# Window attention in front of two gated layers on one Trainium2 core: the first batch's attention, with scores two items ahead, later scaling and an earlier release

## The chip, the cores and the metric

The kernel runs on 1 core of a Trainium2 chip. The metric is the time of one execution on the device, in microseconds; three runs of the kernel before stand in the table below. The engines are called PE (TensorE, matrix products into PSUM banks), PEld (PE's weight loads), DVE (VectorE), ACT (ScalarE), POOL (GpSimd) and SP (SyncE, which issues the transfers).

## The reference

Three stages follow each other; each one's output is the next one's input.

```python
# q, k, v: (4 batches, 8 heads, 576 rows, 64)
rel = pos[:, None] - pos[None, :]
bias = slopes[:, None, None] * (-np.abs(rel).astype(np.float32))[None, :, :]
mask = (rel >= 0) & (rel < window)            # window = 128
scores = np.where(mask, scale * q @ k.T + bias, -1e9)
attn = np.exp(scores - scores.max(-1)); attn = attn / (attn.sum(-1) + 1e-09)
x = (attn @ v)                                # to (2304, 512)
...
g = x @ w_gate                                # 512 -> 1536
silu = g * (1.0 / (1.0 + np.exp(-g)))
x = silu * (x @ w_val) @ w_out
...
h = x @ w_in2                                 # 512 -> 2048
out = (h * np.cos(h)) @ w_out2
```

The weights of the last two stages come in 64 bits and are turned into float32 on the chip; products use a high and a low part of each operand (`wh`, `wl`, `xh`, `xl`), three matmuls for one.

## The kernel before

The instructions of all engines are written out in program order by one Python loop, and each engine works its own queue in that order; waits are set by tile. The loop over `n` runs through 144 *items* of attention: 16 units (4 batches of 4 pairs of heads, `u`), each of 9 items, which are blocks of 128 rows (four for either head, `i` = 0 to 3, and a tail of 64 rows for both heads together). Two neighbouring items form a group, `first` and `final` are its first and last place. For each item these steps stand in the loop at fixed lags:

- `do_s`: scores by PE into a bank of the pool `s` (two banks), in bursts of two groups at places 0 and 4 of a unit and the tail at place 7 (`AHEAD`); each burst needs K and q of its unit, transposed by PE (`prep_t`, lines L401 and L413, into the bank `pq` or `t`) and copied into SBUF by DVE or ACT (`prep_q` L407, `prep_k` L410, `prep_tail` L421 and L423).
- `do_bias` (L471, DVE): adds the slope and forms the row maximum, from PSUM into `e`.
- `do_exp` (L480, ACT): the exponential with its row sum, two items behind the first of the group.
- `do_guard` and `do_recip` (L486 and L491, DVE) on the row sums, and `do_norm` (L503 and L504, POOL): scaling, `NORM` = 2 items behind the group's last.
- `do_t` (L513 and L523, PE): transposes, 5 behind; `do_hi` (L541 and L536, ACT): copies out of PSUM, 6 behind; `do_pv` (L576, and L554 and L556 for the tail, PE): product with v, 8 behind for the blocks, 9 for the tail. Its end writes `xh` (ACT, L581 and L563) and `xl` (DVE, L582 and L565).

When the fourth pair of a batch has its tail's `xl`, `release` frees the batch for the *filler*: matmuls of the gated layer for the first three slices of 128 of its 1536 columns (`a_l1`, `a_l2`, lines L81 to L83 into the pool `pm`, two banks). `run_fill` puts 1.6 steps of three matmuls each into every item. Until the first release there is nothing to fill in. In program order the first release falls at item 45.

The weights of these slices, nine blocks of 512 columns, are converted during the first batch: `convert` loads a block (L92, L97), ACT makes two parts of it (L123, L125), DVE clamps, shifts and joins them (L126, L133, L134), DVE or POOL adds (L138 or L143), ACT or POOL makes the high part `wh` (L165, L170), POOL the low part `wl` (L158).

Behind the attention the rest of the filler, the other slices of the gated layer and the cosine layer follow; their code is not changed.

Of the kernel before, what the change touches and what calls it, by code (L numbers as in the profile page):

```python
# [28 lines left out]
def kernel(  # L29
# [70 lines left out]
    def convert(dst, todo, fast=False, act=False):  # L100
# [9 lines left out]
        added = set()  # L110
        for i, (key, src, f, column, pool) in enumerate(todo):
# [3 lines left out]
            if act and i + 1 < len(todo):  # L115
                stages.append(load_stage(*todo[i + 1][1:4]))
# [3 lines left out]
            if wide:  # L120
                t = conv_p.tile([128, 512], F32, tag="ct", name="ct")
                r = st[:, :, 0]
                nc.scalar.activation(out=t, in_=st[:, :, 1].bitcast(F32), func=AF.Abs, scale=65536.0)  # L123
                yield
                nc.scalar.activation(out=r, in_=r, func=AF.Copy, scale=2.0 ** -29)  # L125
                nc.vector.tensor_scalar(t, t, LEAST_HIGH, GREATEST_HIGH, ALU.max, ALU.min)  # L126
                yield
# [3 lines left out]
            if wide:  # L131
                ti = t.bitcast(U32)
                nc.vector.tensor_scalar(ti, ti, 3, None, ALU.logical_shift_left)  # L133
# [98 lines left out]
    def evac_l1(nm, f, st, ps):  # L232
        if nm == "g":
# [94 lines left out]
    s_p = att.enter_context(tc.tile_pool(name="s", bufs=8))  # L328
# [51 lines left out]
    load_qk(1)  # L380
    load_v(0)
# [3 lines left out]
    for t in qtx:  # L385
        nc.vector.memset(t, 0.0)
    pth = {}
# [21 lines left out]
    def prep_k(u):  # L409
        nc.vector.tensor_copy(out=KT[u][:, :NB * 128], in_=PQ.pop((u, "k")))  # L410
# [5 lines left out]
    def prep_tail(u):  # L416
        ps = PQ.pop((u, "t"))
        KT[u] = qk_p.tile([128, S], F32, tag="kx", name="kx")
# [21 lines left out]
    def do_s(groups):  # L440
# [36 lines left out]
    def do_exp(n):  # L477
        w = width(items[n][2])
        e, (st, m) = E[n], ST[n]
        nc.scalar.activation(out=e[:, :w], in_=e[:, :w], func=AF.Exp, bias=st[:, m:m + 1], scale=-1.0,  # L480
                             accum_out=st[:, 2 + m:3 + m])

    def do_guard(g):
        st = ST[g[0]][0]
        c = len(g)
        nc.vector.tensor_scalar(st[:, 4:4 + c], st[:, 2:2 + c], 1e-9, None, ALU.add)  # L486

    def do_recip(g):
        st = ST[g[0]][0]
        c = len(g)  # L490
        nc.vector.reciprocal(out=st[:, 6:6 + c], in_=st[:, 4:4 + c])  # L491
# [6 lines left out]
    def do_norm(n):  # L498
# [5 lines left out]
        nc.gpsimd.tensor_scalar(e[:, :w], e[:, :w], st[:, 6 + m:7 + m], 1.0, ALU.mult, ALU.mult)  # L504
# [108 lines left out]
    EXP, NORM, TRANS, HIGH, PVS = 2, 2, 5, 6, 8  # L613
    AHEAD = {0: (0, 2), 4: (4, 6), 7: (8,)}
    Q0, K0, TT0 = 2, 5, 4
    due = pdue = 0.0
    for n in range(N + PVS + 2):
# [11 lines left out]
        if ended(HIGH):  # L629
            do_hi(ended(HIGH))  # L630
# [4 lines left out]
        if ended(NORM):  # L635
            do_guard(ended(NORM))
        if ended(TRANS):
            do_t(ended(TRANS))
        if v1 is not None:
            if idx == TT0:  # L640
                g = ended(TRANS)
                prep_tail_t(v1, TT[g[0]] if g else ps_t.tile([128, 512], F32, tag="t", name="t"))
        if ended(NORM):
            do_recip(ended(NORM))
            for m in ended(NORM):
# [5 lines left out]
        for back in (PVS, PVS + 1):  # L651
            for m in (ended(back) or ())[-1:]:
                u_, h_, i_ = items[m]
                if back == PVS and h_ == 1 and i_ == NB - 1 or back == PVS + 1 and i_ == NB:
                    do_pv(m)
        if v1 is not None:
# [10 lines left out]
            if idx == max(TT0, K0) + 1:  # L667
# [555 lines left out]
```

## Time and profile before

| | |
|---|---|
| runs | 993.61 us median of 3 (993.47 to 993.85) |
| the profiled execution | 993.59 us, span 991.6 us |
| PE busy | 968.4 us (98%), 5616 instructions |
| DVE, ACT, POOL busy | 745.7 us (75%), 587.0 us (59%), 477.9 us (48%) |
| mean granted clock of PE | 0.984 |
| chain that ended last | PE 89%, DVE 4%, ACT 2% |

The span runs from the first to the last instruction; the execution's own time is some 2 us longer. An engine's busy share is an average over stages that differ: the profile's slices show PE's clock at 0.7 to 0.8 in the first three of forty and at the full value in those behind. [...]

### The profile page before, as it was taken

To read this page: it belongs to the slowest core of one execution; us is meant where nothing else is said; L and a number is where in the kernel's file an instruction comes from. 1 tells how busy PE (TensorE), PEld (TensorE's weight loads), DVE (VectorE), ACT (ScalarE), POOL (GpSimd) and SP (SyncE) were. 2 spreads that over 40 slices of the span, in tenths; PEclk is the share of its full clock that TensorE was granted. 3 is DMA by queue.
4 is the path that set the end of the run, shared out by engine and by line. 5 is a ranking of instruction groups with operands and counts; after the bars stand their busy time and mean duration, and the time that the engine had idled before them with its cause. 6 is when DMAs were issued, how large, how long until landed. Compare 5 with 4: busy or idle time off the path is not lost.

```text
span 991.6 us, 17044 instructions
## 1 busy us (share of the span) xinstructions
PE 968.4 (98%) x5616; PEld 888.0 (90%) x5616; DVE 745.7 (75%) x1560; ACT 587.0 (59%) x1349; POOL 477.9 (48%) x563
## 2 busy tenths in 40 slices
PE   5889999999999999999999999999999999999998
PEld 3568888889999999999999999888889888898886
DVE  6978877866288988989989755889666796666664
ACT  5876666554244545555555433877677776776663
POOL 4766556642245667669679720344222342223221
PEclk8879999999999999999999999999999999999999
DMA  7533333222373646647557625765767656676552
GB/s 180 139 100 73 97 79 91 72 80 70 106 282 106 202 128 216 209 128 251 172 165 242 203 81 174 285 202 176 249 199 229 200 162 200 184 242 200 164 177 85
DMA packets 145159, 163.65 MB, mean 165 GB/s; under 512 B 64688, under 2 KB 105648, under 8 KB 144816
## 3 DMA queue, kind: packets, MB, share of 16 engines
q1 hardware_dynamic: 143872, 162.27, 52.5%
q8 instruction: 45, 0.74, 0.3%
q10 hardware_dynamic: 1200, 0.30, 0.1%
q14 instruction: 42, 0.34, 0.1%
HBM read 126.88 MB, written 35.65 MB: 164 GB/s over the span
## 4 chain that ended last, share of the span: by engine, by line
PE 89%; DVE 4%; ACT 2%; issue 1%; DMA 1%; POOL 1%; SPq 1%; POOLq 0%; DVEq 0%; ACTq 0%
PE l L81 13%; PE l L83 13%; PE l L82 13%; PE pm L81 8%; PE pm L83 7%; PE pm L82 7%; PE pm L946 6%; PE pm L948 5%; PE pm L947 5%; PE s L463 4%; PE pv L576 3%; PE t L523 1%; PE pq L401 1%; PE t L513 1%; DVE cs L765 1%
## 5 line engine op out<-in xcount | busy, mean ns | idle before, releaser
L1071 POOL TENSOR_TENSOR r<-r,c 128x384 f32<-128x384 f32 x96 | 104.2, 1087 | 261.9 <-ACT r L1069 174.8
L81 PE MATMUL pm<-xh,wh 128*128 128x384 f32 (+1 forms) x452 | 150.9, 334 | 0.0
L83 PE MATMUL pm<-xh,wl 128*128 128x384 f32 (+1 forms) x452 | 144.8, 320 | 0.0
L82 PE MATMUL pm<-xl,wh 128*128 128x384 f32 (+1 forms) x452 | 144.6, 320 | 0.0
L81 PE MATMUL l<-wo,hh 128*128 128x512 f32 x288 | 113.9, 395 | 0.0
L82 PE MATMUL l<-wo,hh 128*128 128x512 f32 x288 | 113.5, 394 | 0.0
L83 PE MATMUL l<-wo,hl 128*128 128x512 f32 x288 | 113.5, 394 | 0.0
L946 PE MATMUL pm<-xh,ws 128*128 128x384 f32 x318 | 107.7, 339 | 0.5 <-ACT q L1097 0.5
L767 POOL TENSOR_TENSOR cs<-cs,st 128x512 uint32<-128x512 uint32 x56 | 79.9, 1427 | 57.6 <-DVE cs L765 48.8
L948 PE MATMUL pm<-xh,ws 128*128 128x384 f32 x318 | 107.6, 338 | 0.0
L947 PE MATMUL pm<-xl,ws 128*128 128x384 f32 x318 | 107.1, 337 | 0.0
L504 POOL TENSOR_SCALAR e<-e,st 128x128 f32<-128x128 f32 (+1 forms) x144 | 60.6, 424 | 63.2 <-DVE st L491 38.9
L81 PEld LDWEIGHTS pm<-xh,wh 128*128 128x128 f32 x452 | 85.1, 188 | 3.2 <-issue 3.2
L82 PEld LDWEIGHTS pm<-xl,wh 128*128 128x128 f32 x452 | 85.3, 189 | 0.0
L83 PEld LDWEIGHTS pm<-xh,wl 128*128 128x128 f32 x452 | 85.0, 188 | 0.0
L1061 ACT ACTIVATE a<-c 128x384 f32<-128x384 f32 x96 | 49.7, 518 | 54.6 <-DVE c L1087 54.6
L1066 DVE SCALAR_TENSOR_TENSOR r<-a,r 128x384 f32<-128x384 f32 x96 | 76.0, 792 | 3.3
L480 ACT ACTIVATE e<-e,st 128x256 f32<-128x256 f32 (+1 forms) x144 | 67.9, 473 | 16.3 <-DVE st L471 12.3
L1068 ACT ACTIVATE r<-r 128x384 f32<-128x384 f32 x96 | 50.3, 524 | 42.7 <-DVE r L1066 42.7
L81 PE MATMUL l<-uh,wh 128*128 128x384 f32 x216 | 72.8, 337 | 0.7 <-DVE acc L892 0.5
L83 PE MATMUL l<-uh,wl 128*128 128x384 f32 x216 | 72.6, 336 | 0.0
L82 PE MATMUL l<-ul,wh 128*128 128x384 f32 x216 | 72.5, 336 | 0.0
(171 smaller groups left out, 2622.6 us busy)
## 6 DMA issues: line engine op xcount, KB each, us to landing
ws<-wid SPq DMA_DIRECT2D x168, 256.0 KB, 2.8
wo<-wod SPq DMA_DIRECT2D x48, 512.0 KB, 5.0
st<-in_moe_w_out_dram SPq DMA_DIRECT2D x28, 512.0 KB, 3.8
st<-in_moe_w_in_dram SPq DMA_DIRECT2D x16, 512.0 KB, 3.7
st<-in_moe_w_gate_dram SPq DMA_DIRECT2D x12, 512.0 KB, 4.1
st<-in_moe_w_val_dram SPq DMA_DIRECT2D x12, 512.0 KB, 4.0
wid<-sh SPq DMA_DIRECT2D x24, 256.0 KB, 4.1
wid<-sl SPq DMA_DIRECT2D x24, 256.0 KB, 3.6
```

The costliest lines, as they stand in the source:

```text
L81: nc.tensor.matmul(out=ps, lhsT=ah, rhs=bh, start=start, stop=False)
L82: nc.tensor.matmul(out=ps, lhsT=ah, rhs=bl, start=False, stop=False)
L83: nc.tensor.matmul(out=ps, lhsT=al, rhs=bh, start=False, stop=stop)
L480: nc.scalar.activation(out=e[:, :w], in_=e[:, :w], func=AF.Exp, bias=st[:, m:m + 1], scale=-1.0, accum_out=st[:, 2 + m:3 + m])
L504: nc.gpsimd.tensor_scalar(e[:, :w], e[:, :w], st[:, 6 + m:7 + m], 1.0, ALU.mult, ALU.mult)
L767: nc.gpsimd.tensor_tensor(out=ti, in0=ti, in1=st[:, :, 0], op=ALU.add)
L946: nc.tensor.matmul(out=o, lhsT=wh, rhs=xh_, start=start and kk == 0, stop=False, skip_group_check=True)
L947: nc.tensor.matmul(out=o, lhsT=wh, rhs=xl_, start=False, stop=False, skip_group_check=True)
L948: nc.tensor.matmul(out=o, lhsT=wl, rhs=xh_, start=False, stop=kk == 1, skip_group_check=True)
L1066: nc.vector.scalar_tensor_tensor(out=r, in0=a, scalar=-C2, in1=r, op0=ALU.mult, op1=ALU.add)
L1068: nc.scalar.activation(out=r, in_=r, func=AF.Abs)
L1071: nc.gpsimd.tensor_tensor(out=r, in0=r, in1=h, op=ALU.mult)
```

## The change

The loop over items stays; what changes is at which item the steps stand, which engine makes one copy, and in which shape some small instructions work.

- Units of the first batch get their scores two items earlier (`bursts`), into four banks: groups take turns between the pool `s` and the pool `pm`, which the filler does not use yet.
- Guard and scaling stand 3 items behind a group's last in place of 2, except for the last pair of the first batch (`staged`), which keeps 2 and has its transposes, copies and products one, one and two items earlier.
- The row statistics lie in ten fixed tiles of 12 columns; sums stand in columns 2 and 4, and the guard and the reciprocal of two items run over three columns, the one between included.
- K is copied by ACT in place of DVE. In the first batch q and K are transposed at places 1 and 3 of a unit in place of 2 and 5, and the next q and k are loaded at place 2 in place of 6.
- The clamp and the shift of a converted block go over even and odd words in turn (`p (c t) -> p t c`); the second block is loaded before the first v.
- Value rows of the filler wait for the silu of their own slice alone.
- In program order the first release falls at item 42.

```diff
@@ convert
         stages = [load_stage(*todo[0][1:4])]
         added = set()
+        if act:
+            yield
+            stages.append(load_stage(*todo[1][1:4]))
...
-                nc.vector.tensor_scalar(t, t, LEAST_HIGH, GREATEST_HIGH, ALU.max, ALU.min)
+                w = t.rearrange("p (c t) -> p t c", t=2) if act else t
+                nc.vector.tensor_scalar(w, w, LEAST_HIGH, GREATEST_HIGH, ALU.max, ALU.min)
...
-                nc.vector.tensor_scalar(ti, ti, 3, None, ALU.logical_shift_left)
+                w = ti.rearrange("p (c t) -> p t c", t=2) if act else ti
+                nc.vector.tensor_scalar(w, w, 3, None, ALU.logical_shift_left)
@@ a_l1, evac_l1
-            while (nm, f) not in g0 or (nm == "v" and "silu" not in st):
+            while (nm, f) not in g0 or (nm == "v" and ("silu", f) not in st):
...
-                if f == F0 - 1:
-                    st["silu"] = True
+                st["silu", f] = True
@@ before the loop
     load_qk(1)
+    next(pieces)
     load_v(0)
...
+    stats = [const.tile([128, 12], F32, name=f"st{j}") for j in range(10)]
+    for t in stats:
+        nc.vector.memset(t, 1.0)
@@ prep_k
-        nc.vector.tensor_copy(out=KT[u][:, :NB * 128], in_=PQ.pop((u, "k")))
+        if u not in KT:
+            KT[u] = qk_p.tile([128, S], F32, tag="kx", name="kx")
+        nc.scalar.copy(out=KT[u][:, :NB * 128], in_=PQ.pop((u, "k")))
@@ do_s
-            ps = ps_s.tile([128, 512], F32, tag="s", name="s")
-            st = s_p.tile([128, 8], F32, tag="st", name="st")
+            if items[g[0]][0] < NP and stat_turn[0] % 2:
+                ps = pm.tile([128, 512], F32, tag="pm", name="pm")
+            else:
+                ps = ps_s.tile([128, 512], F32, tag="s", name="s")
+            st = stats[stat_turn[0] % len(stats)]
+            stat_turn[0] += 1
@@ do_guard, do_recip
-        c = len(g)
-        nc.vector.tensor_scalar(st[:, 4:4 + c], st[:, 2:2 + c], 1e-9, None, ALU.add)
+        c = 2 * len(g) - 1
+        nc.vector.tensor_scalar(st[:, 5:5 + c], st[:, 2:2 + c], 1e-9, None, ALU.add)
...
-        nc.vector.reciprocal(out=st[:, 6:6 + c], in_=st[:, 4:4 + c])
+        nc.vector.reciprocal(out=st[:, 8:8 + c], in_=st[:, 5:5 + c])
@@ the loop over items
-    EXP, NORM, TRANS, HIGH, PVS = 2, 2, 5, 6, 8
-    AHEAD = {0: (0, 2), 4: (4, 6), 7: (8,)}
-    Q0, K0, TT0 = 2, 5, 4
+    EXP, NORM, TRANS, HIGH, PVS = 2, 3, 5, 6, 8
+    bursts = {}
+    for u in range(U):
+        when = (-2, 2, 5) if u < NP else (0, 4, 7)
+        for at, js in zip(when, ((0, 2), (4, 6), (8,))):
+            bursts.setdefault(max(u * NI + at, 0), []).extend(first[u * NI + j] for j in js)
+    TT0 = 4
...
+    def last_pair(n):
+        return 0 <= n < N and items[n][0] == NP - 1
+    def staged(n, late, early):
+        if last_pair(n - early) and n - early in final:
+            return final[n - early]
+        return None if last_pair(n - late) else final.get(n - late)
...
+        Q0, K0 = (1, 3) if u < NP - 1 else (2, 5)
...
+        normal, turned, high = staged(n, NORM, 2), staged(n, TRANS, 4), staged(n, HIGH, 5)
...
-        if u < U and idx in AHEAD:
-            do_s([first[u * NI + j] for j in AHEAD[idx]])
+        if n in bursts:
+            do_s(bursts[n])
...
-        for back in (PVS, PVS + 1):
+        for back in (PVS + 1, PVS, PVS - 2):
...
-                if back == PVS and h_ == 1 and i_ == NB - 1 or back == PVS + 1 and i_ == NB:
+                if (h_ == 1 and i_ == NB - 1 or i_ == NB) and back == (
+                        PVS - 2 if last_pair(m) else PVS if i_ == NB - 1 else PVS + 1):
                     do_pv(m)
...
-            if idx == max(TT0, K0) + 1:
+            if idx == (2 if u < NP - 1 else 6):
                 load_qk(u + 2)
```

Line numbers of the changed kernel are higher by 4 to 15 in this part: the clamp is L130, the shift L138, the bias L486, the guard L501, the reciprocal L506, the scaling L519, the copy of K L420.

At the start SP's queue holds the transfers in this order (`st` is a weight block in its staging buffer). Before:

```order
L92 DMA st<-in_moe_w_gate_dram 128x4x256
L348 DMA q<-in_q_dram 128x4x64 x2
L348 DMA k<-in_k_dram 128x4x64 x2
L353 DMA qkt<-in_q_dram 64x2x64
L353 DMA qkt<-in_k_dram 64x2x64
L364 DMA v<-in_v_dram 128x4x64 x2
L368 DMA vtail_128<-in_v_dram 64x2x64
L92 DMA st<-in_moe_w_val_dram 128x4x256
```

and in the changed kernel:

```order
L92 DMA st<-in_moe_w_gate_dram 128x4x256
L351 DMA q<-in_q_dram 128x4x64 x2
L351 DMA k<-in_k_dram 128x4x64 x2
L356 DMA qkt<-in_q_dram 64x2x64
L356 DMA qkt<-in_k_dram 64x2x64
L92 DMA st<-in_moe_w_val_dram 128x4x256
L367 DMA v<-in_v_dram 128x4x64 x2
L371 DMA vtail_125<-in_v_dram 64x2x64
```

The block of w_val has moved ahead of the three transfers of the first v.

On DVE, where a pair's output and a weight block are worked on in the middle of the first batch (`st` statistics, `ct` a block in conversion, `xl` the low part of the output), the order before is:

```order
L471 ISA e,st<-s,relt,slope 128x192
L471 ISA st 128x1
L582 TENSOR_TENSOR xl<-pv,xh 128x512
L126 TENSOR_SCALAR ct<-ct 128x512
L486 TENSOR_SCALAR st<-st 128x2
L491 RECIPROCAL st<-st 128x2
L565 TENSOR_TENSOR xl<-pq,xh 64x64 x2
L133 TENSOR_SCALAR ct<-ct 128x512
L134 SCALAR_TENSOR_TENSOR ct<-st,ct 128x512
```

and in the changed kernel:

```order
L486 ISA e,st_175<-pm,relt,slope 128x192
L486 ISA st_175 128x1
L501 TENSOR_SCALAR st_173<-st_173 128x3
L506 RECIPROCAL st_173<-st_173 128x3
L597 TENSOR_TENSOR xl<-pv,xh 128x512
L130 TENSOR_SCALAR ct<-ct 128x2x256
L580 TENSOR_TENSOR xl<-pq,xh 64x64 x2
L138 TENSOR_SCALAR ct<-ct 128x2x256
L139 SCALAR_TENSOR_TENSOR ct<-st,ct 128x512
```

The guard has moved in front of both `xl`, over three columns, and the clamp and the shift go over two runs of 256 words.

On PE, from the end of the last output product of the first batch's fourth pair to the first matmul of the filler, the order before is:

```order
L576 MATMUL pv<-pth_859,v 64x128
L463 MATMUL s<-kx,qt_163 128x192
L513 MATMUL t<-ident,e 128x128 x2
L554 MATMUL pq<-ptt,v 128x128
L556 MATMUL pq<-ptt,vtail_128 128x128
L463 MATMUL s<-kx,qx 128x128 x2
L463 MATMUL s<-kx,qx 128x256 x2
L81 MATMUL pm<-xh,wh 128x288
```

and in the changed kernel:

```order
L591 MATMUL pv<-pth_838,v 64x128
L569 MATMUL pq<-ptt,v 128x128
L571 MATMUL pq<-ptt,vtail_125 128x128
L409 MATMUL pq<-ident,k 128x128 x4
L528 MATMUL t<-ident,e 128x128 x2
L81 MATMUL pm<-xh,wh 128x288
```

The tail's scores and the next unit's first burst now stand behind the first filler matmuls, and four transposes of K in front of them. In all 204 in place of 211 matmuls stand in PE's queue ahead of the first filler matmul.

## Rows read from the trace of the kernel before

**Rows 1.** Windows: us, PE, PEld, DVE, ACT, POOL busy (instructions), clock, DMA share, GB/s.

```profile
7.00:72.50 65.50, 54.91 (x281) 36.79 (x281) 55.26 (x186) 49.61 (x154) 43.54 (x64) 0.77 0.56 141
...
74.00:210.00 136.00, 136.00 (x1071) 116.54 (x1068) 107.87 (x437) 85.27 (x307) 80.20 (x189) 1.00 0.33 81
```

**Rows 2.** Chain that ended last, 60 to 76 us: start us, us, what.

```profile
61.64 1.29 issue
...
72.45 0.52 PE s L463 x2
72.97 0.22 PE t L513 x2
...
73.64 0.87 PE s L463 x8
74.51 0.33 PE pm L81
...
75.11 0.14 PE pm L81
```

**Rows 3.** Windows, as in rows 1, around one fall of the clock.

```profile
47.50:51.00 3.50, 1.64 (x12) 1.01 (x10) 3.35 (x9) 2.40 (x8) 2.02 (x3) 1.00 0.80 219
51.50:57.50 6.00, 6.00 (x24) 4.10 (x25) 5.86 (x18) 5.81 (x19) 4.88 (x7) 0.50 0.51 140
```

**Rows 4.** Timeline of DVE and POOL: start us, us, instruction [idle before <-releaser].

```profile
22.92 1.58 POOL L158 TENSOR_TENSOR wl<-ct,wh 128x512 fp32r<-128x512 f32 x1
23.85 0.14 DVE L486 TENSOR_SCALAR st<-st 128x1 f32<-128x1 f32 x1
...
44.94 0.16 DVE L486 TENSOR_SCALAR st<-st 128x2 f32<-128x2 f32 x1
...
60.49 1.56 POOL L158 TENSOR_TENSOR wl<-ct,wh 128x512 fp32r<-128x512 f32 x1
...
61.12 0.95 DVE L486 TENSOR_SCALAR st<-st 128x2 f32<-128x2 f32 x1 [0.20 <-ACT e L480]
...
62.38 0.46 DVE L565 TENSOR_TENSOR xl<-pq,xh 64x64 fp32r<-64x64 f32 x2
```

**Rows 5.** Chain that ended last, 8 to 16 us: start us, us, what.

```profile
8.50 0.59 SPq L364
...
10.33 4.14 DMA st<-in_moe_w_val_dram
```

**Rows 6.** Lines of DVE, 7 to 72.5 us: busy us, mean ns | idle before, releaser.

```profile
L486 DVE TENSOR_SCALAR st<-st 128x2 f32<-128x2 f32 x19 | 8.2, 430 | 1.4 <-ACT e L480 1.2
...
L126 DVE TENSOR_SCALAR ct<-ct 128x512 f32<-128x512 f32 x9 | 4.8, 537 | 2.2 <-ACT ct L123 2.2
L133 DVE TENSOR_SCALAR ct<-ct 128x512 uint32<-128x512 uint32 x9 | 4.5, 503 | 0.3
L407 DVE TENSOR_SCALAR qx<-pq,qscale 128x512 f32<-128x512 f32 x6 | 4.4, 734 | 4.6 <-PE pq L401 4.6
...
L410 DVE COPY kx<-pq 128x512 f32<-128x512 f32 x5 | 3.4, 686 | 1.4 <-PE pq L401 1.4
```

**Rows 7.** Lines of ACT, 7 to 72.5 us, same columns.

```profile
L480 ACT ACTIVATE e<-e,st 128x256 f32<-128x256 f32 x28 | 13.9, 498 | 0.5 <-DVE st L471 0.3
...
L541 ACT COPY pth<-t 128x512 f32<-128x512 f32 x8 | 4.6, 577 | 1.5 <-PE t L523 1.4
L480 ACT ACTIVATE e<-e,st 128x128 f32<-128x128 f32 x10 | 4.0, 403 | 5.2 <-DVE st L471 5.2
L421 ACT ACTIVATE qt<-t,qscale 64x64 f32<-64x64 f32 x12 | 3.7, 312 | 2.5 <-PE t L413 2.4
...
L423 ACT COPY kx<-t 128x64 f32<-128x64 f32 x6 | 1.3, 212 | 0.1
```

**Rows 8.** Timeline of DVE, first weight blocks.

```profile
15.65 0.43 DVE L133 TENSOR_SCALAR ct<-ct 128x512 uint32<-128x512 uint32 x1
16.11 0.69 DVE L134 SCALAR_TENSOR_TENSOR ct<-st,ct 128x512 uint32<-128x512 uint32 x1
```

More of the change, by code (lines that the diff above doesn't have):

```diff
@@ L114, in convert @@
                 yield
-            if act and i + 1 < len(todo):
+            if act and len(stages) < i + 2 <= len(todo):
                 stages.append(load_stage(*todo[i + 1][1:4]))
@@ L327 @@
     e_p = att.enter_context(tc.tile_pool(name="e", bufs=7))
-    s_p = att.enter_context(tc.tile_pool(name="s", bufs=8))
     ps_s = att.enter_context(tc.tile_pool(name="ps_s", bufs=2, space=PSUM))
@@ L386 @@
         nc.vector.memset(t, 0.0)
+    stats = [const.tile([128, 12], F32, name=f"st{j}") for j in range(10)]
+    for t in stats:
+        nc.vector.memset(t, 1.0)
+    stat_turn = [0]
     pth = {}
@@ L417, in prep_tail @@
         ps = PQ.pop((u, "t"))
-        KT[u] = qk_p.tile([128, S], F32, tag="kx", name="kx")
+        if u not in KT:
+            KT[u] = qk_p.tile([128, S], F32, tag="kx", name="kx")
         for j in range(2):
@@ L480, in do_exp @@
         nc.scalar.activation(out=e[:, :w], in_=e[:, :w], func=AF.Exp, bias=st[:, m:m + 1], scale=-1.0,
-                             accum_out=st[:, 2 + m:3 + m])
+                             accum_out=st[:, 2 + 2 * m:3 + 2 * m])
     def do_guard(g):
         st = ST[g[0]][0]
-        c = len(g)
-        nc.vector.tensor_scalar(st[:, 4:4 + c], st[:, 2:2 + c], 1e-9, None, ALU.add)
+        c = 2 * len(g) - 1
+        nc.vector.tensor_scalar(st[:, 5:5 + c], st[:, 2:2 + c], 1e-9, None, ALU.add)
     def do_recip(g):
         st = ST[g[0]][0]
-        c = len(g)
-        nc.vector.reciprocal(out=st[:, 6:6 + c], in_=st[:, 4:4 + c])
+        c = 2 * len(g) - 1
+        nc.vector.reciprocal(out=st[:, 8:8 + c], in_=st[:, 5:5 + c])
     def folded(n):
@@ L503, in do_norm @@
             nc.gpsimd.tensor_tensor(out=e[:, :w], in0=e[:, :w], in1=e[:, w:2 * w], op=ALU.add)
-        nc.gpsimd.tensor_scalar(e[:, :w], e[:, :w], st[:, 6 + m:7 + m], 1.0, ALU.mult, ALU.mult)
+        nc.gpsimd.tensor_scalar(e[:, :w], e[:, :w], st[:, 8 + 2 * m:9 + 2 * m], 1.0, ALU.mult, ALU.mult)
     def do_t(g):
@@ L620 @@
         v1 = u + 1 if u + 1 < U else None
+        Q0, K0 = (1, 3) if u < NP - 1 else (2, 5)
         def ended(j):
             return final.get(n - j)
+        normal, turned, high = staged(n, NORM, 2), staged(n, TRANS, 4), staged(n, HIGH, 5)
         todo = list(post)
         post.clear()
-        if u < U and idx in AHEAD:
-            do_s([first[u * NI + j] for j in AHEAD[idx]])
-        if ended(HIGH):
-            do_hi(ended(HIGH))
+        if n in bursts:
+            do_s(bursts[n])
+        if high:
+            do_hi(high)
         for m in first.get(n - EXP, ()):
@@ L634 @@
             do_bias(m)
[L635 to L638, printed above, removed]
+        if normal:
+            do_guard(normal)
+        if turned:
+            do_t(turned)
         if v1 is not None:
             if idx == TT0:
-                g = ended(TRANS)
+                g = turned
                 prep_tail_t(v1, TT[g[0]] if g else ps_t.tile([128, 512], F32, tag="t", name="t"))
-        if ended(NORM):
-            do_recip(ended(NORM))
-            for m in ended(NORM):
+        if normal:
+            do_recip(normal)
+            for m in normal:
                 do_norm(m)
```

## The prediction

> **What bounds the kernel now.** I read the windows by stage first. From 74 to 210 us TensorE (PE) is busy without a gap at the full clock, and it stays the bound behind that; before 72.5 us it is busy 54.91 of 65.50 us at a mean granted clock of 0.77, and VectorE (DVE) is the fullest engine with 55.26 us, 84.4% [rows 1]. So the kernel has two parts: a first one in which the attention of batch 0 runs alone, since the filler (the gated layer's matmuls) has no input yet, and a second in which PE is full and every microsecond of PE work counts. The seam is the first filler matmul at 74.51 us [rows 2]. What the change is worth is how much earlier this seam comes, less the PE work that it pushes behind the seam.
>
> The chain of waits shows what holds the first part. It runs through PE nearly all the way, with holes: at 61.64 us PE stands 1.29 us before it may transpose the next q [rows 2]. That transpose writes the bank pq, which the tail's output occupies until DVE has formed xl; DVE does so at 62.38 us, after its guard (the `+1e-9` on the row sums, two columns) took 0.95 us in place of the 0.16 of an undisturbed one. The guard ended with GpSimd's (POOL) 1.56 us instruction on wl, which had begun before it [rows 4]. A guard of one column went through in 0.14 us under the same POOL line [rows 4]. Over the first part the 19 guards of two columns took 8.2 us, 430 ns each [rows 6]; at 0.166 they are 3.2, so about 5.0 us are waiting for POOL.
>
> [...]
>
> Fourth, the start: the second weight block, w_val, is issued at 10.33 us and lands 4.14 us later [rows 5]; its first DVE instruction waits 2.2 us for it through ScalarE (ACT) [rows 6], with the bias blocks of later items queued behind it.
>
> **The change part by part.** *Copies of K to ACT.* DVE loses six copies at 686 ns [rows 6], 4.1 us. ACT up to the cast of xh of the fourth pair gets five; the nearest ACT row is the 128x512 copy out of PSUM, 577 ns, so +2.9. Counted on the order up to that cast, ACT also has two 256-wide exponentials (498 ns), two qt (312) and one kx tail (212) fewer, -1.8 [rows 7]. Its busy time goes from 49.61 to 50.7 us; on DVE 55.3 becomes 51.2.
>
> *Guard.* One guard-and-reciprocal pair fewer stands ahead of the seam, -0.3. The others cover three columns; no row shows three. Bounds: as the one-column row, 0.14 us, or as the two-column rows, 430 ns with the waits. I take the first, because the only odd width in the trace passed under POOL's instruction: -5.0, DVE 45.9; the other end leaves 50.9.
> [...]
>
> *Strided halves.* The 18 DVE instructions L126 and L133 write every second word, in two passes. Contiguous they take 0.43 us undisturbed [rows 8], 537 and 503 ns with waits [rows 6]. Bounds: 0.43 as now, or 0.69 as L134, which handles the same 512 elements and reads every second word [rows 8]: 18 x 0.26 = +4.7, less the 1.6 us of waits in today's rows if POOL no longer delays them, +3.1. I take no change, since L134 shows the stride itself free for a read; both ends are kept.
>
> *Scores two items ahead, in four banks; q and K earlier; loads at place 2.* The number of matmuls is the same. The bias blocks find their scores ready, and PE need not wait for a bank. On ACT, 5.2 us of idle stand before 128-wide exponentials that wait for DVE's bias [rows 7]. I book no term for this; it is what lets the fullest engine stay as full as now although the load is shared more evenly. The loads of q and k move ahead of a weight block in the SP queue; that block is needed an item group later, which hides the six issues. If not, DVE would stand as it does now at the start, 2.2 us [rows 6].
>
> *The start.* w_val is issued before the three transfers of v, at about 8.50 instead of 10.33 us [rows 5]: -1.8 us of DVE's 2.2 us wait. The v loads, then later, are read only by the first output product. Ten small memsets are added where DVE stands idle 4.6 us in front of its first q [rows 6].
>
> *Scaling an item later.* For pairs 0 to 2 the guard stands one item further behind the exponentials, so that DVE need not wait for ACT; the transposes stay where they were. Pair 3 keeps the old lags up to the scaling, and is transposed, copied and multiplied one, one and two items sooner.
>
> *Release at item 42.* In program order the last output product moves from item 42 to 40 and the tail from 44 to 41. Ahead of the first filler matmul PE loses a tail score (0.52), a burst of scores (0.87) and two transposes (0.22) [rows 2]: 1.6 us go behind the seam. Between the last product and the seam stand two tail products and six transposes, some ten records of 0.11 us [rows 2], 1.1 us; now it is 2.0 (72.5 to 74.51).
>
> *Sum.* ACT, with 50.7 us, becomes the fullest. As today's share I take DVE's without the startup wait, 55.26 / (65.5 - 1.8) = 86.7%: 50.7 / 0.867 = 58.5, so the cast comes at 7.0 + 58.5 = 65.5 us, the seam at 66.6, 7.9 us earlier. Less 1.6 of moved PE work: 6.3. The value rows wait for the silu of their own slice alone, so the two items without filler that the old order has (52 and 53) go; PE has no gap there now [rows 1], hence no term. Released earlier at the same rate, the filler runs out of work at items 79 and 80: at most 2 x 1.6 steps of three matmuls of 0.14 us [rows 2], 1.3; attention fills PE in between, so I take 0.2. The profiled execution took 993.59 us (span 991.6 and 2.0 around it; the median of the runs, 993.61, is the same): 993.59 - 6.3 + 0.2 = 987.5 us.
>
> **The rivals.** *DVE is not relieved* (still locked, or strided at 0.69, or both): DVE has 49.0 to 54.0 us. At 50.9 it ties with ACT, and the exponentials go on waiting as now; with today's whole share, 50.9 / 0.844 = 60.3, the seam is at 68.4, gain 4.5: 989.3 us. With both, 54.0 / 0.867 = 62.3, seam 70.4, gain 2.5: 991.3. For it: rows of width 2. Against: the row of width 1.
>
> [...] PE's 54.91 us at 0.77 [rows 1] are 42.3 at full clock. More even waits may let the clock fall more often: at a mean of 0.66 they are 64 us, all of the old time, and the gain shrinks to what the release gives, 0 to 2 us: 992 to 993.6. For it: the fall behind a half-idle stretch [rows 3]. Against: that stretch holds the wait for pq and the wait for a bank of scores, which the change aims at.
>
> *Slower: a strided write is expensive.* Place: L126 and L133, nine blocks, all ahead of the seam and in front of bias blocks. The seam plus 1.6 us must not pass 74.51, so the cast not 71.8: 64.8 x 0.867 = 56.2 us of DVE, 10.3 above 45.9, 0.57 for each of 18. The kernel is slower from 1.0 us an instruction; at 1.38, twice L134's, DVE has 63.0, the cast comes at 79.7, the seam at 80.8, 7.9 later with the moved work: 1001.5 us. Against: L134's read.
> [...] No run here shows a write with a step of two.
>
> *More than I book:* with scores always ready ACT could be 95% full: 53.4 us, seam at 61.5, gain 11.4: 982.4 us.
>
> **How the numbers follow.** The sum above 0.47; DVE not relieved 0.27; PE at 1.2 GHz 0.12; strided write expensive 0.06; more than booked 0.08. 0.2% is 2 us, about what a measurement of this kernel can tell from no change. Faster than 991.6: 0.47, 0.08, 0.25 of the second and 0.04 of the third, 0.84; within 0.2%: 0.10; slower 0.06. The range runs from the good case, 982.4, to the start of the PE rival, 992; the bounds of the guard (5.0 us) and the stride (+3.1) lie inside.
>
> **What would show it.** The first filler matmul near 66.6 us; guards of three columns at 0.2 us while POOL works (over 0.4: still locked); L130 and L138 at 0.43; DVE's wait for w_val under 0.6 us; the clock in the first part at 0.77 or more; PE without gaps behind the seam, or holes of up to 0.6 us at items 79 and 80; everything behind shifted by the same amount. I am wrong if ACT is far from full in the first part, if the first filler matmul finds xl of pair 3 missing, or if the clock is at 0.50 when the filler starts, which alone costs up to half of such a stretch, 3 us.

## The result

The changed kernel takes 1000.25 us (median of 4 runs, 999.12 to 1001.53), the kernel before 993.54 beside it; the ratio is 1.0069 with a 95% interval of 1.0052 to 1.0087. I had forecast 987.5. The profiled execution took 999.12 us (span 997.4), 5.5 more than that of before.

Windows of the changed kernel, in the stretches and columns of [rows 1]:

```profile
7.00:72.50 65.50, 47.96 (x277) 30.88 (x275) 53.06 (x175) 52.37 (x162) 41.36 (x61) 0.87 0.60 146
74.00:210.00 136.00, 135.07 (x1046) 114.22 (x1046) 100.57 (x413) 88.07 (x309) 77.86 (x182) 1.00 0.31 76
```

The granted clock is a share of PE's full clock: in windows of 0.5 us up to 75 us of the kernel before it is 1.00 or 0.50, and between them only where it changes. As an estimate, the work that PE does, in time at the full clock, is busy time times mean clock. Up to 72.5 us that is 47.96 x 0.87 = 41.7 us, and 54.91 x 0.77 = 42.3 before [rows 1]. By the same estimate PE loses less to its lower level (6.2 in place of 12.6 us) and about as much more to idle time (17.5 in place of 10.6). My sum counted ACT and DVE up to the cast of `xh` of the fourth pair, which comes at 69.89 us, not 65.5. The window up to there:

```profile
7.00:69.89 62.89, 47.36 (x274) 30.48 (x273) 52.37 (x174) 49.82 (x152) 40.58 (x60) 0.86 0.61 148
```

ACT has 49.82 us, near the 50.7 that I had booked, but fills only 79% of the stretch and not 86.7%. DVE, the engine to be relieved, has 52.37 us, not 45.9, and is still the fullest (83%).

The chain of waits around the seam, as [rows 2]:

```profile
67.52 2.33 PE pv L591 x16
69.85 0.42 PE pq L569 x2
70.26 0.24 PE pq L571 x2
70.50 2.75 issue
73.25 0.63 PE pq L409 x4
73.88 0.22 PE t L528 x2
74.10 0.13 PE pm L81
```

The fourth pair's product begins 2.4 us earlier than before (69.94), but a hole of 2.75 us stands behind its tail, so the first filler matmul comes at 74.10, 0.4 us earlier and not 7.9. What fills the hole is seen on ACT and DVE (timeline: start, us, instruction):

```profile
70.38 0.63 ACT L432 ACTIVATE qt<-t,qscale 64x64 f32<-64x64 f32 x2
...
71.02 0.21 ACT L434 COPY kx<-t 128x64 f32<-128x64 f32 x1
71.26 0.51 ACT L495 ACTIVATE e<-e,st 128x256 f32<-128x256 f32 x1
...
71.77 0.49 ACT L495 ACTIVATE e<-e,st 128x256 f32<-128x256 f32 x1
...
72.26 0.41 ACT L578 CAST xh<-pq 64x64 fp32r<-64x64 f32 x2
72.70 0.46 DVE L580 TENSOR_TENSOR xl<-pq,xh 64x64 fp32r<-64x64 f32 x2 [1.49 <-ACT xh L578]
```

The tail's output lies ready in the bank `pq` from 70.5 us on, but ACT first does the next pair's q and K tails and two exponentials. K's transposes (L409) need that bank and stand ahead of the filler in PE's queue.

What PE waits for, 7 to 72.5 us (engine, line, releaser: us in total, times, longest), after and then before:

```profile
PE t L538 <- POOL e L519: 14.5, 16, 2.1
```

```profile
PE s L463 <- DVE st L471: 4.2, 3, 2.7
...
PE t L523 <- POOL e L504: 2.1, 3, 1.0
```

PE no longer waits for scores' banks; it waits seven times as long for POOL's scaling ahead of the transposes. The same wait shows behind the seam. Lines of PE, 75 to 235 us, after and then before:

```profile
L528 PE MATMUL t<-ident,e 128*128 128x128 f32 x94 | 20.7, 281 | 1.8 <-POOL e L519 1.4
```

```profile
L513 PE MATMUL t<-ident,e 128*128 128x128 f32 x92 | 17.5, 272 | 0.0
```

94 transposes at the price of before (17.5 / 92) are 17.9 us; 20.7 is 2.8 more, and 1.8 of idle time come to it: 4.6 us. With 0.4 gained at the seam and some 1.5 of moved work that is 5.7, about the 5.5 us measured. Against the forecast the profiled execution is 11.6 us late: 7.5 of it stand ahead of the seam (74.10 and not 66.6), 4.1 behind it.

The lines of DVE, 7 to 72.5 us, as [rows 6], and K on ACT, as [rows 7]:

```profile
L130 DVE TENSOR_SCALAR ct<-ct 128x512 f32<-128x512 f32 x9 | 7.4, 818 | 4.7 <-ACT ct L126 4.7
L501 DVE TENSOR_SCALAR st<-st 128x3 f32<-128x3 f32 x18 | 6.9, 385 | 0.7 <-ACT e L495 0.7
...
L143 DVE CUSTOM_DVE_ANT_0 ct<-st,ct 128x1024 uint16<-128x1024 uint16 x4 | 5.2, 1308 | 0.0
...
L138 DVE TENSOR_SCALAR ct<-ct 128x512 uint32<-128x512 uint32 x9 | 4.1, 459 | 0.2
```

```profile
L420 ACT COPY kx<-pq 128x512 f32<-128x512 f32 x4 | 2.3, 578 | 0.0
```

The guard of three columns takes 385 ns, not 140. The timeline of DVE and POOL, as [rows 4], shows why, and that clamp and add wait in the same way:

```profile
28.22 1.27 POOL L163 TENSOR_TENSOR wl<-ct,wh 128x512 fp32r<-128x512 f32 x1
...
28.52 1.52 DVE L143 CUSTOM_DVE_ANT_0 ct<-st,ct 128x1024 uint16<-128x1024 uint16 x1
...
37.98 1.31 POOL L148 TENSOR_TENSOR ct<-ct,st 128x512 uint32<-128x512 uint32 x1
...
38.75 0.82 DVE L130 TENSOR_SCALAR ct<-ct 128x512 f32<-128x512 f32 x1 [0.82 <-ACT ct L126]
...
59.46 1.27 POOL L163 TENSOR_TENSOR wl<-ct,wh 128x512 fp32r<-128x512 f32 x1
...
59.63 1.12 DVE L501 TENSOR_SCALAR st<-st 128x3 f32<-128x3 f32 x1 [0.72 <-ACT e L495]
```

The guard ends at 60.75, 0.02 behind POOL's 60.73; the clamp 0.28 behind, the add 0.55 behind. The shape is not to blame: undisturbed, the strided clamp (L130) and shift (L138) take what the whole shift took in [rows 8], and the whole clamp beside it (last line, the kernel before):

```profile
9.07 0.43 DVE L130 TENSOR_SCALAR ct<-ct 128x512 f32<-128x512 f32 x1 [1.62 <-ACT ct L126]
9.54 0.43 DVE L138 TENSOR_SCALAR ct<-ct 128x512 uint32<-128x512 uint32 x1
```

```profile
15.19 0.43 DVE L126 TENSOR_SCALAR ct<-ct 128x512 f32<-128x512 f32 x1 [2.18 <-ACT ct L123]
```

### The profile page after: what moved, and what is told of

It is laid out like the page before. It is cut to its first block, busy times and chain, and to the rows that moved or that the text cites. A ratio compares the mean times of both kernels' runs of the same rounds, so it can differ in the third digit from the quotient of the medians.

```text
span 997.4 us, 17040 instructions
## 1 busy us (share of the span) xinstructions
PE 965.1 (97%) x5616; PEld 882.3 (88%) x5616; DVE 741.5 (74%) x1554; ACT 594.3 (60%) x1365; POOL 477.7 (48%) x563
## 4 chain that ended last, share of the span: by engine, by line
PE 86%; DVE 4%; ACT 3%; POOL 2%; DMA 2%; issue 2%; SPq 1%; POOLq 0%; DVEq 0%; ACTq 0%
PE l L81 13%; PE l L83 13%; PE l L82 13%; PE pm L81 7%; PE pm L83 7%; PE pm L82 7%; PE pm L979 5%; PE pm L981 5%; PE pm L980 5%; PE s L478 3%; PE pv L591 3%; POOL e L519 1%; PE t L528 1%; PE pq L409 1%; PE t L538 1%
## 5 line engine op out<-in xcount | busy, mean ns | idle before, releaser
L519 POOL TENSOR_SCALAR e<-e,st 128x128 f32<-128x128 f32 (+1 forms) x144 | 60.0, 421 | 81.3 <-DVE st L506 33.0
L82 PE MATMUL l<-ul,wh 128*128 128x384 f32 x216 | 72.5, 336 | 0.0
```

Of the source, the lines that this page charges most:

```text
L82: nc.tensor.matmul(out=ps, lhsT=ah, rhs=bl, start=False, stop=False)
L519: nc.gpsimd.tensor_scalar(e[:, :w], e[:, :w], st[:, 8 + 2 * m:9 + 2 * m], 1.0, ALU.mult, ALU.mult)
```

## The experiments

In the diffs, - is the changed kernel and + the experiment, unless another base is named. Times are medians; the kernel before, run beside them, had medians of 993.1 to 993.5, and 992.4 beside the last two. A ratio is to those runs, with its 95% interval. Where two experiments did not run beside each other, the difference of their medians and that of their ratios need not agree; I give both where it matters.

### Where the time behind the seam goes, and what the single edits do

**e1_scale2: scaling 2 items behind again, outside the first batch.**

```diff
+        normal = {m + (3 if items[m][0] < NP - 1 else 2): g for m, g in final.items()}.get(n)
```

> The changed kernel, but from the second batch on guard and scaling stand 2 items behind a group's last again (as before); the first batch keeps 3. Theory A (behind the seam the later scaling makes PE's pair transposes wait for POOL: about 11 of them stretched by 0.1 to 0.8 us, 3.5 us in all, and smaller waits beside): these waits go, the seam stays at 73.9 us, and the time falls by 3.5 to 4.5 us, to 996 to 997. Rival B (POOL or ACT is late there for another reason, such as the copies of K on ACT): the waits stay, within 1 us of 1000.

Measured: 996.18 us, ratio 1.0036 (1.0024 to 1.0049). The lines of PE, 75 to 235 us:

```profile
L528 PE MATMUL t<-ident,e 128*128 128x128 f32 x94 | 18.2, 273 | 0.6 <-POOL e L519 0.6
```

The stretched transposes are gone, and 4.1 us with them by the medians (3.3 by the ratios to the kernel before). Theory A.

**f1_b_scale3: the kernel before, with this one edit.**

```diff
-    EXP, NORM, TRANS, HIGH, PVS = 2, 2, 5, 6, 8
+    EXP, NORM, TRANS, HIGH, PVS = 2, 3, 5, 6, 8
```

> The kernel before with guard and scaling 3 items behind a group's last in place of 2, nothing else. Theory A (this lag alone makes PE's pair transposes wait for POOL, everywhere): idle time and stretched transposes behind the seam as in the changed kernel, 3.5 to 4.5 us, and no gain in the first part: 996.5 to 998. Rival B (it costs only together with the other edits, such as the copies of K on ACT): within 1 us of 993.3.

Measured: 997.23 us, ratio 1.0042 (1.0030 to 1.0055), 4.1 us slower. PE's waits up to 74 us:

```profile
PE t L523 <- POOL e L504: 12.9, 13, 2.1
```

Alone, too, the later scaling costs what its removal gave back. Theory A. (The waits are those of its slowest execution, 999.54 us.)

**e2_guard1: the guard as instructions of one column.**

```diff
-        c = 2 * len(g) - 1
-        nc.vector.tensor_scalar(st[:, 5:5 + c], st[:, 2:2 + c], 1e-9, None, ALU.add)
+        for c in range(0, 2 * len(g), 2):
+            nc.vector.tensor_scalar(st[:, 5 + c:6 + c], st[:, 2 + c:3 + c], 1e-9, None, ALU.add)
```

> The changed kernel with the guard of a group as two instructions of one column each in place of one over three columns. Theory A (a guard of three columns waits for POOL's instruction to end, 8 of 18 up to the seam, and DVE's lateness is what keeps the first part long): each one-column guard takes 0.13 us also under POOL, the guards up to the seam fall from 6.9 us to about 4.7, the seam comes 1 to 2 us earlier, and some of the waits of PE behind it go too: 997 to 999. Rival B (the wait is only moved to DVE's next instruction, or lies off the path): seam at 73.9, 1000.

Measured: 1002.33 us (999.92 to 1002.89), ratio 1.0095 (1.0081 to 1.0109). Lines of DVE, 7 to 72.5 us:

```profile
L130 DVE TENSOR_SCALAR ct<-ct 128x512 f32<-128x512 f32 x9 | 9.2, 1027 | 5.1 <-ACT ct L126 5.1
...
L501 DVE TENSOR_SCALAR st<-st 128x1 f32<-128x1 f32 x40 | 4.3, 142 | 0.2 <-ACT e L495 0.2
```

The guards of one column show no wait for POOL (142 ns in the mean of 40), as I had read from [rows 4]; the clamp then waits longer (1027 ns), and nothing is gained: the time is no better than the 1000 us of Rival B.

**e3_whole: clamp and shift in one pass.**

```diff
-                w = t.rearrange("p (c t) -> p t c", t=2) if act else t
+                w = t
-                w = ti.rearrange("p (c t) -> p t c", t=2) if act else ti
+                w = ti
```

> The changed kernel with the clamp and the shift of a converted block over all words in one pass, as before. Theory A (the strided passes take 0.43 us as the whole ones do, and wait for POOL as the whole ones do; the 818 ns of the clamp are waits that depend on what POOL does then): the clamp stays near 0.8 us, no change, 999 to 1001. Rival B (the strided clamp is what became slower, 818 against 537 ns): the clamp falls to 0.54 us, DVE saves 2.5 us, seam 2 us earlier, 998.

Measured: 1001.03 us (997.89 to 1004.29), ratio 1.0085 (1.0067 to 1.0104). The whole clamp takes 897 ns with its waits. Theory A: the shape neither costs nor helps.

**e4_tailnow: the fourth pair's tail copies right behind its product.** The release stands in the same function, so it moves from item 42 to 41 with them, here and in every experiment that keeps this edit.

```diff
-            post.append(fin)
+            if u == NP - 1:
+                fin()
+            else:
+                post.append(fin)
```

> The changed kernel with the copies of the fourth pair's tail output (xh on ACT, xl on DVE) issued right behind its product, ahead of the q and k tail copies and two exponentials that now stand in front of them on ACT. Theory A (the hole of 2.75 us on PE ahead of the seam is the bank pq waiting for these copies, 1.6 to 2 us of it for ACT's queue): xh of the tail at 70.5 in place of 72.3, seam at 72.0 to 72.4, time 998 to 998.8. Rival B (the filler then waits for something else, the biases or K): seam not before 73.5, 1000.

Measured: 999.73 us, ratio 1.0075 (1.0061 to 1.0088). In its chain the hole is shorter by 1.7 us:

```profile
72.60 0.24 PE pq L571 x2
72.83 1.04 issue
73.87 0.63 PE pq L409 x4
```

The mechanism is there, but this execution came to the hole 2.3 us later, and the time does not tell it apart from no change. **f3_tailnow2** makes the same edit on e5_scale2_all (below):

> e5_scale2_all (996.15 us) with the fourth pair's tail copies right behind the product, as in e4_tailnow, where the hole ahead of the seam fell from 2.75 to 1.04 us and the time by 0.5. Theory A (the hole is worth its length): 994 to 995. Rival B (the time goes to a wait behind it): 996.

Measured: 994.57 us (991.53 to 996.98), ratio 1.0015 (1.0003 to 1.0027), 1.6 us less than its base. That is Theory A's time, but not the hole's length alone: the seam comes 0.9 us earlier in the profile (72.31, and 73.23 in e5_scale2_all), and the rest lies behind it, where PE has a granted clock of 1.00 here and of 0.50 there (the 72 to 76 us windows here and below):

```profile
72.00:76.00 4.00, 4.00 (x32) 3.83 (x32) 2.14 (x12) 3.40 (x12) 1.82 (x5) 1.00 0.73 163
```

What the copies alone are worth stays open.

### Is the first part bound by the load of an engine?

**e5_scale2_all: scaling 2 items behind everywhere.**

```diff
-    EXP, NORM, TRANS, HIGH, PVS = 2, 3, 5, 6, 8
+    EXP, NORM, TRANS, HIGH, PVS = 2, 2, 5, 6, 8
```

> The changed kernel with guard and scaling 2 items behind a group's last everywhere, the first batch too (e1_scale2 changed it back behind the first batch alone, 996.18 us). Theory A (the later scaling costs PE waits wherever it stands, since it leaves two items in place of three between POOL and the transposes): the first part shortens too, seam 1 to 2 us before that of e1_scale2, 994 to 995.5. Rival B (in the first batch it spares DVE its waits for ACT's exponentials, 1.2 us, and more behind them): seam later, 997 to 998. Rival C: neither, 996.

Measured: 996.15 us, as e1_scale2: Rival C. Its profile shows a gain given back: the fourth pair's product starts at 65.8 us, but behind the hole ahead of the filler PE runs at a granted clock of 0.50, as in [rows 3] (windows, columns as above):

```profile
70.00:72.00 2.00, 0.28 (x2) 0.31 (x3) 0.80 (x3) 1.12 (x6) 0.45 (x1) 0.73 0.64 145
72.00:76.00 4.00, 4.00 (x18) 4.00 (x17) 0.77 (x6) 1.57 (x5) 1.58 (x4) 0.50 0.57 130
```

The hole alone does not decide this. It is 2.75 us long here, as in the changed kernel, where the full clock stands behind it:

```profile
70.50:73.25 2.75, 0.00 (x0) 0.03 (x1) 1.20 (x4) 2.10 (x9) 0.46 (x1) 1.00 0.49 110
74.10:76.00 1.90, 1.90 (x17) 1.90 (x16) 0.59 (x3) 1.39 (x5) 0.00 (x0) 1.00 0.59 134
```

**e6_k_dve: e1_scale2 with K copied by DVE.**

```diff
-        nc.scalar.copy(out=KT[u][:, :NB * 128], in_=PQ.pop((u, "k")))
+        nc.vector.tensor_copy(out=KT[u][:, :NB * 128], in_=PQ.pop((u, "k")))
```

> e1_scale2 (996.18 us) with the copies of K on DVE again. In the first part ACT is busy 36.3 of the 40 us from 20 to 60, DVE 35.6. Theory A (both are nearly full and wait for each other, so that work carried from one to the other gives nothing): within 1 us of 996. Theory B (ACT is the bound, the copies cost there): seam 2 to 3 us earlier, 993 to 994. Theory C, that of the prediction (DVE is the bound): seam 3 to 4 us later, 999 to 1000.

Measured: 999.26 us, but spread from 995.63 to 1000.37; ratio 1.0055 (1.0038 to 1.0072). The median speaks for C, by 3.1 us (1.9 by the ratios), but with this spread it does not decide; h1_k_dve, on a steadier base, does not bear C out.

**e7_less_act and e8_less_dve: e1_scale2 with work left out.**

```diff
-                nc.scalar.activation(out=r, in_=r, func=AF.Copy, scale=2.0 ** -29)
+                if act:
+                    r = zero
+                else:
+                    nc.scalar.activation(out=r, in_=r, func=AF.Copy, scale=2.0 ** -29)
```

```diff
-                nc.vector.tensor_scalar(w, w, LEAST_HIGH, GREATEST_HIGH, ALU.max, ALU.min)
+                if not act:
+                    nc.vector.tensor_scalar(w, w, LEAST_HIGH, GREATEST_HIGH, ALU.max, ALU.min)
```

> e1_scale2 (996.18 us) without ACT's scaling of the low words of the nine blocks (9 x 0.68 us; a tile of zeros is added in their place, so the low words of the weights are left out). Theory A (ACT and DVE together): 1 to 3 us of the 6.1 come back at the seam, 993 to 995. Theory B (ACT is the bound): 5 to 6 us, 990 to 991. Theory C (DVE is the bound): no change, 996.

> e1_scale2 (996.18 us) without DVE's clamp of the nine blocks (9 x 0.82 us with its waits for POOL; the limits on the exponents are left out). Theory A (ACT and DVE together): 1 to 3 us of the 7.4 come back at the seam, 993 to 995. Theory B (ACT is the bound): no change, 996. Theory C (DVE is the bound): 6 to 7 us, 989 to 990.

Measured: 996.20 us (993.07 to 996.81) and 997.04 us (994.72 to 998.28). Windows of the two, the first part, from executions 3.1 and 1.6 us under these medians:

```profile
7.00:72.50 65.50, 46.60 (x285) 30.18 (x284) 54.60 (x179) 47.48 (x153) 41.64 (x61) 0.90 0.61 146
```

```profile
7.00:72.50 65.50, 46.32 (x279) 30.23 (x278) 46.72 (x169) 52.66 (x162) 41.46 (x61) 0.87 0.60 147
```

ACT falls to 47.48 us, DVE to 46.72, near the 45.9 that I had forecast for it, and by the medians neither shortens the kernel: on this base Theory B for DVE's clamp, C for ACT's scaling, and A's 1 to 3 us on neither side. Neither engine by itself is the bound.

### The same questions with the clock held

**f2_b_warm and f4_warm: matmuls on zeros where PE waits.** Base of the first is the kernel before (2 matmuls a group), of the second f3_tailnow2 (3).

```diff
+        for _ in range(3 if u < NP else 0):
+            nc.tensor.matmul(out=ps, lhsT=warm[:, :128], rhs=warm, start=True, stop=True)
```

> The kernel before with two matmuls on a tile of zeros (128x512, 0.22 us each at full clock) ahead of each of the 20 groups of transposes of the first batch, where PE now waits; their output is overwritten. [...] Theory A (PE's half-speed stretches, which follow its idle ones, hold the first part): the mean clock up to the seam rises from 0.77 to over 0.9 and the seam comes 3 to 8 us earlier, 986 to 990. Theory B (the first part is a chain across the queues of four engines, in which PE's speed matters little): the clock rises, the time stays within 1.5 us of 993.3. Theory C (the added matmuls stand in the way): 995 to 999.

> f3_tailnow2 with three matmuls on a tile of zeros ahead of each of the 20 groups of transposes of the first batch, where PE waited 7.6 us for POOL in e5_scale2_all; their output is overwritten. Theory A (half-speed stretches of PE behind its idle ones hold the first part and the start of the filler; 10.9 us were lost to the lower level in e5_scale2_all): clock over 0.9 up to the seam, 4 to 8 us less than f3_tailnow2. Theory B (chain across the queues): as f3_tailnow2, within 1.5 us. Theory C (they stand in the way): 2 to 6 us more.

Measured: 991.13 us (990.68 to 992.13), ratio 0.9983 (0.9975 to 0.9992), and 991.35 us (990.58 to 991.48), ratio 0.9985 (0.9976 to 0.9993). For the length of one added matmul, those of 128x512 in the kernel before start 0.23 us apart at a clock of 1.00 (950.00 to 950.93). The first part of f2_b_warm and of f4_warm:

```profile
7.00:72.50 65.50, 60.02 (x337) 41.10 (x337) 57.74 (x194) 51.68 (x163) 45.54 (x65) 1.00 0.56 144
```

```profile
7.00:72.50 65.50, 56.38 (x358) 40.30 (x356) 51.66 (x183) 53.58 (x164) 42.40 (x61) 0.97 0.63 149
```

With the clock up, and net of what the added matmuls take, the kernel before gains 2.0 us and the changed one's variant 3.2. In the first PE loses 12.6 us to the lower level by [rows 1], so most of that loss lay in time in which PE would have waited anyway: Theory B for the larger part, A for the rest. f4_warm falls short of its Theory A's 4 us too. With the clock held, the runs of one kernel spread over 0.8 to 2.6 us (f2, f4 and those below) in place of 1.7 to 6.4 in the experiments above, so differences of 1 to 2 us begin to show on this base.

**g2_less_act and g3_less_dve: the two reliefs again, on f4_warm.**

> f4_warm (991.35 us) without ACT's scaling of the low words of the nine blocks (9 x 0.68 us; a tile of zeros is added, so the low words of the weights are left out). Theory A (at full clock the first part is a chain across the queues of all engines): 0 to 1.5 us less. Theory B (ACT, 34.9 us busy of the 40 from 20 to 60, is the bound): 5 to 6 us less, 985 to 986.

> f4_warm (991.35 us) without DVE's clamp of the nine blocks (0.5 to 0.8 us each with its waits; the limits on the exponents are left out). Theory A (chain across the queues): 0 to 1.5 us less. Theory B (DVE, 34.3 us busy of the 40 from 20 to 60, is the bound): 4 to 6 us less, 986 to 987.

Measured: 989.19 us (988.47 to 991.11), and 991.14 us (989.53 to 991.95). ACT gives back 2.2 of its 6.1 us (2.3 by the ratios), between A and B; DVE 0.2 (0.7), Theory A.

**g5_scale3_first: the later scaling in the first batch alone, on f4_warm** (`NORM` is 2 there; the added line is that of e1_scale2).

> f4_warm (991.35 us) with guard and scaling 3 items behind a group's last in the pairs 0 to 2 of the first batch, as in the changed kernel, and 2 behind that. Theory A (the later scaling makes PE wait for POOL in the first batch too, 13 to 15 us in place of some 7): seam 1 to 3 us later, 992.5 to 994.5. Theory B (what PE waits there is other queues' time anyway): within 1 us.

Measured: 992.52 us (991.06 to 993.60), 1.2 more (0.6 by the ratios), with 5.9 us of PE's waits for POOL ahead of the transposes in place of 1.4. That is the lower end of Theory A's time, but the seam comes only 0.3 us later (70.90, and 70.56 in f4_warm): most of these waits take the place of others, as Theory B has it.

**g6_not_ahead: the old bursts, on f4_warm.**

```diff
-            if items[g[0]][0] < NP and stat_turn[0] % 2:
+            if False:
...
-        when = (-2, 2, 5) if u < NP else (0, 4, 7)
+        when = (0, 4, 7)
...
-        Q0, K0 = (1, 3) if u < NP - 1 else (2, 5)
+        Q0, K0 = 2, 5
...
-            if idx == (2 if u < NP - 1 else 6):
+            if idx == 6:
```

> f4_warm (991.35 us) with the scores of the first batch in the old bursts (places 0, 4 and 7), two banks, q and K at places 2 and 5 and the loads at place 6. Theory A (the earlier scores are what lets the first part run 1.7 us shorter than in f2_b_warm): seam 1.5 to 4 us later, 993 to 995. Theory B (they give nothing, as the waits move elsewhere): within 1 us.

Measured: 989.98 us (989.73 to 990.49), ratio 0.9967 (0.9956 to 0.9979). Neither theory: without the earlier scores, and the earlier q, K and loads that go with them, it is faster by 1.4 us (1.8 by the ratios). The edits were undone together, so which of them costs is not shown.

**h1_k_dve and h2_release45: on g6_not_ahead, K on DVE again (the edit of e6_k_dve), and the old lags of the fourth pair.**

```diff
-        return 0 <= n < N and items[n][0] == NP - 1
+        return False
```

> g6_not_ahead (989.98 us) with the copies of K on DVE again. At full clock taking 6.1 us from ACT gave 2.2 us (g2_less_act), taking the clamp from DVE 0.2 (g3_less_dve). Theory A (ACT is the fuller one now, so the move costs): 2.9 us off ACT and 4.1 on DVE, 0.5 to 1.5 us less, 988.5 to 989.5. Theory B (DVE, as the prediction had it): 2 to 4 us more, 992 to 994.

> g6_not_ahead (989.98 us) with the fourth pair at the lags of the others, so that the first release falls at item 45 in program order as before. Theory A (the early release brings the seam forward, but most of it is PE work put behind the seam): seam 2 to 3 us later, of which 1.6 come back; 990.3 to 991.5. Theory B (it is worth what the seam moves): 992 to 993. Theory C (worth nothing): 990.

Measured: 990.35 us (989.26 to 991.19), ratio 0.9976 (0.9967 to 0.9984): between the two theories, and K's place makes no difference that can be told. And 989.18 us (988.49 to 989.90), ratio 0.9972 (0.9961 to 0.9983). By the medians that is 0.8 us less than g6_not_ahead, by the ratios 0.5 more, and the intervals overlap: the early release gains nothing that these runs can tell (Theory C is the nearest), and whether it costs is open. The release does not fall at item 45 here but at 44, and at 41 in the base, since the tail copies of e4_tailnow were kept. The chain of h2_release45 has no hole ahead of the seam, and the seam comes at 67.84 us, not later but 1.0 earlier than in the base, with the tail's scores in front of it and the next unit's burst behind:

```profile
66.59 0.52 PE s L480 x2
67.11 0.22 PE t L530 x2
67.33 0.28 PE pq L573 x2
67.62 0.22 PE pq L575 x2
67.84 0.14 PE pm L81
```

With g6_not_ahead (0.33%) this is the fastest version here that leaves no work out, 0.28% under the kernel before. It keeps of the change the early w_val, K on ACT, the strided halves, the fixed statistics tiles and the silu by slice; together with the tail copies and a third matmul on zeros these are worth 1.9 us against f2_b_warm (991.13), or 1.1 by the ratios.

## Why the prediction was wrong

- **The step that failed most** is the sum's scaling: "As today's share I take DVE's without the startup wait ... 50.7 / 0.867 = 58.5". It lets the first part shrink with the busy time of its fullest engine. ACT's busy time came out as booked (49.82 us), the share did not (79%), so the cast came at 69.89 us and not 65.5. Nor was ACT the fullest: DVE kept 52.37 us. And no engine's load was the bound: taking 6.1 us off ACT or 7.4 us off DVE changed nothing that the medians tell (e7, e8); with the clock held, 2.2 and 0.2 us came back (g2, g3). What fits these four runs is a chain that passes through the in-order queues of four engines, in which another waits for what one engine saves; which waits make it up was not shown link by link.
- **The later scaling, "the transposes stay where they were", had no term.** That they stay is the cost: two items are left in place of three between POOL's scaling and PE. 4.1 us behind the seam (e1), 4.1 on the kernel before (f1), 0.6 to 1.2 in the first batch at a steady clock (g5). This is the largest term that I had not booked; without it the changed kernel is still 2.9 us slower than before (3.6 by the ratio), in place of 6.7. About half of that is the moved work: in the profile of e1 the seam comes at 74.78, 0.3 later than before, and the stretch behind it is 1.5 us longer.
- **The guard: wrong end of its bounds.** Three columns wait for POOL as two do, 385 against 430 ns in the mean; a single column takes 142 (e2). Of the 18 guards of three columns up to 72.5 us, seven begin under a POOL instruction (L148, L163 or L175), take 0.56 to 1.12 us and end 0.02 to 0.03 behind it. That three columns would pass as one does was my estimate from the one odd width in [rows 4]; why one column passes and three do not was not shown. The rival "still locked", in which the guards go on waiting for POOL, held: DVE was not relieved. But its gain of 4.5 us did not come, and guards that do not wait gained nothing (e2).
- **The strided halves: right** at 0.43 us, undisturbed, for a write with a step of two. The slower rival, with over 1.0 us for such an instruction, came within 1.3 us of the result, by luck: its mechanism did not happen. The clamp's 818 ns are waits for POOL, in either shape (e3).
- **The start: right, and given back.** ACT gets w_val at 12.73 us in place of 14.49 (DVE waits 0.97 for it, not under 0.6). But the next block, w_gate, is the one that q and k were moved ahead of: SP issues it at 15.14 us in place of 11.89, and ACT waits 1.9 us for it. That it "is needed an item group later, which hides the six issues" did not hold. DVE's waits ahead of the clamp sum to 4.7 us, in place of 2.2. (SP, then ACT, in the changed kernel:)

```profile
15.14 0.54 SPq L92 DMA_DIRECT2D st<-in_moe_w_gate_dram  x1
19.97 0.67 ACT L126 ACTIVATE ct<-st 128x512 f32<-128x512 f32 x1 [1.90 <-DMA st<-in_moe_w_gate_dram]
```

- **The seam 1.1 us behind the cast: mis-sized.** It is 4.2 (69.89 to 74.10), 2.75 of it the hole. ACT's queue, in which the copies of the tail's output stand behind other work, was not looked at.
- **Scores two items ahead** were booked as what keeps the fullest engine full. With the earlier q, K and loads they cost 1.4 us (g6). Why is not settled: in f4_warm PE waits 2.2 us ahead of the matmuls on zeros for ACT's `pth` copies, which g6_not_ahead does not show, but no run took that wait away alone.
- **The early release** pushes PE work behind the seam as booked, and gains nothing that can be told (h2): with the old lags the seam even came 1.0 us earlier, without the hole.
- **The clock.** The rival called "PE at 1.2 GHz", with its chance of 0.12, is that of a clock that falls more often. No run shows a frequency; the traces show the clock as a share, with 0.50 as the lower level. It did not happen: the mean rose to 0.87 where the rival had 0.66, and the time saved went into idle PE. That a wait of PE brings the lower level behind it was my reading of [rows 3], and so are the 3 us that a clock of 0.50 at the filler's start was to cost, half of the 6.00 us there. The runs agree in one case: 0.50 from 72 to 76 us in e5_scale2_all, behind two microseconds in which PE was busy for 0.28. They do not in another: 1.00 behind the equally long hole of the changed kernel. So it is true of some waits only, and what decides it was not shown.

The edits undone one after another, each on its base, by the medians: scaling behind the seam 4.1, tail copies 1.6, clock 3.2, earlier scores 1.4, release 0.8, 11.1 us from 1000.25 to 989.18 us (9.6 by the ratios). They are not independent (the tail copies gave 0.5 on the changed kernel itself, within its noise), so the shares hold for this order; that of the release is not clear of noise, and that of the tail copies holds a part of the clock.

## What to carry to other kernels

Where several engines are some 75 to 85% busy (here ACT 79% and DVE 83% up to 69.89 us) and each waits for the others, busy time need not be a bound: take work away from one engine in a trial before counting on moving it. A step that is delayed to spare one engine a wait takes its slack from the next one (4.1 us here, e1 and f1); write down the lag between every producer and consumer before and after. Before an edit that moves work by a microsecond is judged, hold TensorE's clock steady, or the spread of the runs can hide the edit (0.8 to 2.6 us here with the clock held, 1.7 to 6.4 without), and run the two versions beside each other.

## What the runs showed of the hardware

- A DVE instruction on three columns that began under POOL's two-input instruction (L163) ended 0.02 us behind it (59.63 to 60.75, POOL until 60.73); those on a single column showed no wait (e2: 142 ns in the mean of 40).
- DVE's add over 128x1024 16-bit values waited in the same way: 1.52 us under POOL's L163 (28.52 to 30.04, POOL until 29.49), and 0.67 in the kernel before, where it began 0.14 us behind the end of POOL's (30.08, POOL until 29.94).
- A one-source DVE instruction over 512 words that reads and writes every second word, in two passes, took 0.43 us undisturbed (9.07 and 9.54 us), as the contiguous one did (15.19 in the kernel before).
- A hole of 2.75 us on PE was followed by a clock of 0.50 in e5_scale2_all and of 1.00 in the changed kernel.
- 40 matmuls on zeros, 128x512 each, held the granted clock at 1.00 through a first part (7 to 72.5 us) that had 0.77 without them (f2), and the runs lay within 990.68 to 992.13 us.
